# An inverse transform whose last stage contracts real and imaginary part at once, with channel-major rows

## The chip, the cores and the metric

The kernel runs on one core of one Trainium2 chip. The metric is the device time of one execution in microseconds; the median of several runs is given. The engines are named as in the profile: PE (matrix products; PEld is its weight loads), DVE (vector), ACT (scalar), POOL (GpSimd) and SP, which here only issues DMAs.

## The reference

Two layers on 2048 positions of 512 channels, each behind a layer norm and with a residual sum. The first is a long convolution whose kernel comes from 128 complex modes for each channel, done by Fourier transforms of length 4096; the second looks up one of 256 experts for each of 32 heads by the best of 16 keys in each of two halves.

```python
def _A_ref(u, log_A_real, A_imag, C_real, C_imag, log_dt, D_skip):
    L = u.shape[1]
    dt = jnp.exp(log_dt)
    A = -jnp.exp(log_A_real) + 1j * A_imag
    C = (C_real + 1j * C_imag) * dt[:, None]
    P = jnp.exp((A * dt[:, None])[:, :, None] * pos[None, None, :])
    K = 2.0 * jnp.einsum("dn,dnl->dl", C, P).real
    Kf, Uf = jnp.fft.rfft(K, 2 * L), jnp.fft.rfft(u_t, 2 * L)
    y = jnp.fft.irfft(Uf * Kf[None, :, :], 2 * L)[:, :, :L]
    ...
    return y + u * D_skip[None, None, :]

def _B_ref(x, w_q, k1, k2, u, v):
    q = jnp.einsum("nd,dhc->nhc", xf, w_q)
    s1, s2 = (jnp.einsum("nhd,ed->nhe", h, k) for h, k in ((q1, k1), (q2, k2)))
    ...                      # top 1 of 16 in each half, expert = 16 * i1 + i2
    act = _gelu(jnp.einsum("nd,nhkd->nhk", xf, ue))
    return jnp.einsum("nhk,nhk,nhkd->nd", g, act, ve)

h = x + _A_ref(_layernorm(x), ...)
h2 = h + _B_ref(_layernorm(h), ...)
```

## The kernel before

All work is added to a plan (`plan.add(engine, cost, function, ...)`): each step has an engine, an estimated cost, what it reads and writes, and the buffers it takes. `Plan.run` is a list scheduler on the host. It picks for each engine, in model time, the step of the highest rank among those that could start, and so writes the order of instructions on each engine; ranks are shifted by group through the weights in `BIAS`. On the chip each engine works off its own order and waits on semaphores. DMAs are issued by SP in such an order too.

**First half: the convolution.** The 512 channels are four quarters `c` of 128, in 32 groups `g` of four channels `d`. Transforms of 4096 are split in two stages over 32 by 64 frequencies. `factors` (POOL) and `tables` (ACT, DVE) make the modes' tables 16 channels at a time; `kgen` contracts them on PE into `kps` (L664), the convolution's kernel. `u_s1` and `k_s1` are the first stage for input and kernel (`stage1`, matmuls `s1u` and `s1k`, L448, evicted by ACT, L451), `u_s2` and `k_s2` the second (`stage2`, `s2yu` and `s2yk`, L465), whose moving operand is read out of a spectrum tile of 32 groups by 32 frequencies `k` by 4 channels. `k_s2` multiplies the spectra on DVE (`prod`, L701, L702, L704); in the last quarter ACT and POOL take a part (`part`, L708, and `rest`, L712). `k_ia` is the inverse's first stage (`ia`, L733), with 32 x 4 rows of frequency and channel; ACT evicts it into `T` (L738). For quarters 0 to 2 `T` is stored to DRAM as `t_d` (L744); the last quarter's stays in SBUF. As filler, `w_piece` folds keys into query weights (`wps`, `wpt`), stored as `w_d`.

**Handover.** The tables' buffers are closed (`turn_over`); the folded weights come back in four quarters `w_q` (L848), which ACT and DVE split into `w_hi` and `w_lo` (L851, L854).

**Second half: blocks of 256 positions, `b` = 0 to 7.** `prefetch` loads the block's part of `t_d` (`Tb`, L926), its constants (`cb`, two loads, L930) and the input (`xt`, L934), each into two buffers. `inverse` is the inverse's last stage (`ib`, L956): for each of 8 positions, two accumulating matmuls (real part, imaginary part) for each of four quarters, whose outputs lie in four column groups of the array. DVE adds the residual into `h` (L963). `center` and `variance` are the layer norm: `mean`, `hc` (L998), and its high and low part `hhi` (ACT, L1002) and `hlo` (DVE, L1006). `scores` multiplies by the weights (`sc`, L1062) and the experts' first vectors (`xu`, L1069), takes maxima (`mx`, `eq`, `kq`) and finds indices with POOL's help (`ks`, L1097, L1099; `ei`, `ef`, `ix`, L1104 to L1108). `select` counts experts by one-hot products (`oh`, `cnt`), weighs the second vectors (`o`, L1216), adds the residual (`ob`) and stores.

An FP32 matmul appears in the profile as two instructions.

Of the kernel before, what the change touches and what calls it, by code (L numbers as in the profile page):

```python
# [27 lines left out]
def view(t, off, dims):  # L28
# [5 lines left out]
BIAS = dict(cen0=483, cen1=-36, cen2=500, cen3=498, cen4=500, cen5=439, cen6=500, cen7=500, e1=216, ia0=470,  # L34
            ia1=333, ia2=6, ia3=40, inv0=452, inv1=500, inv2=309, inv3=479, inv4=407, inv5=104, inv6=64,
            inv7=500, k100=77, k101=254, k102=489, k103=419, k110=-5, k111=397, k112=327, k113=500, k120=481,
            k121=-358, k122=-122, k123=500, k130=500, k131=-78, k132=467, k133=497, k20=-230, k21=480, k22=500,
            k23=472, par=1000, par0=1000, par1=800, pre0=-182, pre1=7, pre2=-132, pre3=347, pre4=388, pre5=-110,
            pre6=273, pre7=456, sc0=363, sc1=495, sc2=488, sc3=434, sc4=110, sc5=462, sc6=277, sc7=500, sel0=14,
            sel1=454, sel2=487, sel3=209, sel4=478, sel5=497, sel6=497, sel7=-92, st=-12, tab0=286, tab1=-16,  # L40
            tab10=-139, tab11=364, tab12=484, tab13=146, tab14=476, tab15=431, tab16=99, tab17=456, tab18=500,
            tab19=227, tab2=273, tab20=435, tab21=459, tab22=-8, tab23=454, tab24=179, tab25=250, tab26=352,
            tab27=492, tab28=232, tab29=450, tab3=69, tab30=498, tab31=453, tab4=233, tab5=500, tab6=399,
            tab7=361, tab8=479, tab9=476, u100=77, u101=488, u102=303, u103=445, u110=500, u111=276, u112=-28,
            u113=492, u120=-167, u121=500, u122=443, u123=451, u130=491, u131=320, u132=-358, u133=491, u20=472,
            u21=207, u22=500, u23=497, var0=500, var1=431, var2=169, var3=336, var4=204, var5=442, var6=-355,
            var7=500, w0=281, w1=458, w2=-87, w3=367, w4=491, w5=362, w6=435, w7=202, wr=-122)
# [121 lines left out]
def kernel(ctx, tc, xa, xb, xt, lar, aim, cre, cim, ldt, dsk, wq, ka, kb, ue, ve,  # L169
# [14 lines left out]
    t_d = dram.tile([P, 8, 3, 2, 256], F32, name="t_d")  # L184
# [102 lines left out]
    def params():  # L287
# [128 lines left out]
        plan.add("SP", 0.1, lambda: nc.sync.dma_start(e_d, e1), r=["e1"], w=["e_d"], t=["e1"], lag=6.0)  # L416
# [23 lines left out]
    def stage1(dst, lhs8, kt, nm, r, tiles, key):  # L440
        for n in range(2):
            job = {}

            def mm(n=n, job=job):
                ps = bank(job, f"{nm}_{n}")
                for g in range(4):
                    for k in range(2):
                        T.matmul(ps[64 * k:64 * k + 64, g, :], lhs8(4 * n + g), c1_s[:, k], start=True, stop=True)  # L448

            def ev(n=n, job=job):  # L450
                A.copy(dst()[:, 8 * kt + 4 * n:8 * kt + 4 * n + 4].rearrange("p g k d -> p g (k d)"), job["ps"])  # L451

            k = plan.add("PE", 0.93, mm, r=r, t=tiles, take="psA", n_mm=16)
            plan.add("ACT", 0.48, ev, w=[key + (kt, n)], t=tiles, give="psA", after=[k])

    def stage2(c, nm, k4, deps, tiles):
# [3 lines left out]
        def mm():  # L460
            y = Q[c][nm]
            ps = bank(job, f"s2{nm}{c}_{k4}")
            for k in range(4):
                kk = 4 * k4 + k
                T.matmul(ps[:, k, :], c2_s[:, kk, :], y[:, :, kk, :], start=True, stop=True)  # L465
# [4 lines left out]
    def u_s1(c, kt):  # L470
# [16 lines left out]
        plan.add("SP", 0.1, load, w=[xs_k], t=[xs_k], lag=3.0)  # L487
# [85 lines left out]
    def factors(i, made):  # L573
# [17 lines left out]
        if i == 16:  # L591
            plan.add("SP", 0.1, e_load, r=["e_d"], w=["E1"], t=["E1"], lag=6.0)
# [97 lines left out]
    def k_s2(c):  # L690
# [3 lines left out]
        for k4 in range(8):  # L694
            job, k = stage2(c, "yk", k4, deps + [("U", c, k4)], tiles)

            def prod(job=job, k4=k4):
                yk, U = Q[c]["yk"], Q[c]["U"]
                pv = job["ps"].rearrange("p k (g d) -> p g k d", d=4)
                uv = U[:, :, 4 * k4:4 * k4 + 4]  # L700
                V.tensor_mul(yk[:, :, 4 * k4:4 * k4 + 4], pv, uv)  # L701
# [4 lines left out]
            def part(job=job, k4=k4):  # L706
                job["ki"] = wk.tile([P, 32, 4, 4], F32, tag="kt", name=f"ki{k4}", bufs=3)
                A.copy(job["ki"][0:64], job["ps"].rearrange("p k (g d) -> p g k d", d=4)[64:128])  # L708

            def rest(job=job, k4=k4):  # L710
                uv = Q[c]["U"][:, :, 4 * k4:4 * k4 + 4]
# [11 lines left out]
    def k_ia(c):  # L723
        plan.group = f"ia{c}"
        deps = [("P", c, k4) for k4 in range(8)]
        for n in range(8):
            job = {}

            def mm(n=n, job=job):
                ps = bank(job, f"ia{c}_{n}")  # L730
                for g in range(4):
                    for s, t in enumerate((Q[c]["yk"], Q[c]["U"])):
                        T.matmul(ps[:, g, :], t[:, 4 * n + g].rearrange("p k d -> p (k d)"), ca_s[:, s, :],  # L733
                                 start=(s == 0), stop=(s == 1))

            def ev(n=n, job=job):
                t_s = tile_of(Q[c], "T", lambda: con.tile([P, 128, 32], F32, tag="T", name=f"T{c}"))
                A.copy(t_s[:, :, 4 * n:4 * n + 4], job["ps"].rearrange("p g m -> p m g"))  # L738

            k = plan.add("PE", 1.80, mm, r=deps + ["ca"], t=[f"yk{c}", f"U{c}", f"T{c}"], take="psA", n_mm=16)  # L740
            plan.add("ACT", 0.55, ev, w=[("T", c, n)], t=[f"T{c}"], give="psA", after=[k])
        if c < 3:
            def store(r):
                nc.sync.dma_start(t_d[:, :, c, r],  # L744
                                  Q[c]["T"][:, 64 * r:64 * r + 64].rearrange("p (b m) g -> p b (m g)", b=8))

            for r in range(2):
                plan.add("SP", 0.1, lambda r=r: store(r), r=[("T", c, n) for n in range(8)], w=[("t_d", c, r)],
                         t=[f"T{c}"], lag=6.0)
# [3 lines left out]
    def w_piece(n):  # L753
# [32 lines left out]
        plan.add("SP", 0.1, load, w=[f"wq{n}"], t=[f"wq{n}"], lag=7.0)  # L786
# [4 lines left out]
        if q == 3:  # L791
            plan.add("SP", 0.1, store, r=[("wh", 4 * hg + j) for j in range(4)], w=[("w_d", hg)], t=[f"wh{hg}"],
# [48 lines left out]
    for q in range(4):  # L841

        if q:
            plan.ring(f"w_q{q}", f"w_q{q - 1}")

        def load(q=q):
            I["q"] = I["pre"].tile([P, 1024], F32, tag="wq", name=f"w_q{q}", bufs=1)
            nc.sync.dma_start(I["q"], w_d[:, q])  # L848

        def high(q=q):  # L850
            A.copy(I["hi"][:, q], I["q"])  # L851

        def low(q=q):
            V.tensor_sub(I["lo"][:, q], I["q"], I["hi"][:, q])  # L854

        plan.add("SP", 0.1, load, r=["pre"] + [("w_d", h) for h in range(8)], t=[f"w_q{q}"], w=[("w_q", q)], lag=6.0)
# [46 lines left out]
    plan.add("SP", 0.1, u_load, w=["u", "v"], lag=6.0)  # L903
# [16 lines left out]
    def prefetch(b):  # L920
# [3 lines left out]
        def load_t():  # L924
            t["T"] = I["pre"].tile([P, 3, 2, 8, 32], F32, tag="T", name=f"Tb{b}")
            nc.sync.dma_start(t["T"].rearrange("p c r m g -> p c r (m g)"), t_d[:, b])  # L926

        def load_c(a):
            t[f"cb{a}"] = I["pre"].tile([P, 4, 2, 128], F32, tag="cb", name=f"cb{b}_{a}")
            nc.sync.dma_start(t[f"cb{a}"], cb[:, 8 * b + 4 * a:8 * b + 4 * a + 4])  # L930
# [5 lines left out]
        for nm, n, fn, r in ((f"Tb", b, load_t, [("t_d", c, k) for c in range(3) for k in range(2)]),  # L936
                             ("cb", 2 * b, lambda: load_c(0), []), ("cb", 2 * b + 1, lambda: load_c(1), []),
                             ("xt", b, load_x, [])):
            k = key(nm, n)
            plan.add("SP", 0.1, fn, r=["pre"] + r, w=[k], t=[k], lag=6.0)  # L940

    def inverse(b):
# [3 lines left out]
        for a in range(2):  # L946
            job, kc = {}, f"cb{2 * b + a}"

            def mm(a=a, job=job):
# [386 lines left out]
```

## Time and profile before

| | us |
|---|---|
| median of 3 runs | 553.86 (552.82 to 553.98) |
| span of the profiled execution, first to last instruction | 549.5 |
| its own time beside the span | not shown on the page |
| PE busy | 471.7 (86%) |
| DVE busy | 418.6 (76%) |
| POOL busy | 325.5 (59%) |
| ACT busy | 296.4 (54%) |

The span is what the rows of the trace add up to; the device time holds what lies around it too. A busy PE in these rows is an engine with at least one product under way; as products overlap, the rate of starts within a group says more than the busy time. Groups of instructions are given as line, engine, operation, output from inputs, shapes and count, then busy us and mean ns of one, then the idle time before them and what ended it.

### The profile page before, as it was taken

To read this page: it belongs to the slowest core of one execution; us is meant where nothing else is said; L and a number is where in the kernel's file an instruction comes from. 1 tells how busy PE (TensorE), PEld (TensorE's weight loads), DVE (VectorE), ACT (ScalarE), POOL (GpSimd) and SP (SyncE) were. 2 spreads that over 40 slices of the span, in tenths; PEclk is the share of its full clock that TensorE was granted. 3 is DMA by queue.
4 is the path that set the end of the run, shared out by engine and by line. 5 is a ranking of instruction groups with operands and counts; after the bars stand their busy time and mean duration, and the time that the engine had idled before them with its cause. 6 is when DMAs were issued, how large, how long until landed. Compare 5 with 4: busy or idle time off the path is not lost.

```text
span 549.5 us, 16597 instructions
## 1 busy us (share of the span) xinstructions
PE 471.7 (86%) x7154; PEld 409.2 (74%) x7154; DVE 418.6 (76%) x698; ACT 296.4 (54%) x580; POOL 325.5 (59%) x339
## 2 busy tenths in 40 slices
PE   0023899989999999879987969999999999999996
PEld 0013788878999989869976968887888887877785
DVE  4999985899969987698537154788869595969975
ACT  5514998958898589829864334244043323323140
POOL 0758999999999999977607003470352515254500
PEclk9999999999999999989999999999999999999989
DMA  7962464672152031501067478300560503010002
GB/s 241 405 245 72 136 201 132 217 253 64 44 181 74 3 97 50 164 4 41 26 217 298 136 280 299 125 1 1 190 234 2 194 24 111 1 41 0 2 39 78
DMA packets 28481, 67.59 MB, mean 123 GB/s; under 512 B 2772, under 2 KB 14296, under 8 KB 28024
## 3 DMA queue, kind: packets, MB, share of 16 engines
q1 hardware_dynamic: 28256, 66.40, 34.8%
q8 instruction: 56, 0.92, 0.7%
q10 hardware_dynamic: 152, 0.13, 0.1%
q14 instruction: 17, 0.14, 0.1%
HBM read 52.50 MB, written 14.02 MB: 121 GB/s over the span
## 4 chain that ended last, share of the span: by engine, by line
PE 40%; DVE 9%; POOL 2%; issue 1%; DMA 1%; ACT 1%; DVEq 0%
PE sc L1062 13%; PE ia L733 6%; PE ib L956 5%; PE o L1216 5%; PE xu L1069 3%; PE cnt L1196 2%; PE s1k L448 1%; DVE eq L1086 1%; DVE mx L1082 1%; DVE oh L1186 1%; PE kps L664 1%; PE bc L1164 1%; DMA cb<-cb 1%; DVE yk L701 1%; POOL ks L1099 1%
## 5 line engine op out<-in xcount | busy, mean ns | idle before, releaser
L531 POOL TENSOR_TENSOR pg<-PS 128x1024 int32<-128x1024 int32 x32 | 68.8, 2152 | 3.6 <-ACT t L618 3.6
L560 POOL TENSOR_TENSOR mg<-TS 128x1024 f32<-128x1024 f32 x32 | 62.6, 1957 | 11.4 <-issue 4.3
L1186 DVE TENSOR_SCALAR oh<-idxb,ec_s 128x2048 bf16<-128x2048 bf16 (+1 forms) x72 | 49.9, 757 | 13.9 <-ACT idxb L1168 12.8
L1097 POOL TENSOR_TENSOR ks<-kq 128x512 f32<-128x512 bf16 x16 | 20.1, 1259 | 55.4 <-DVE kq L1091 54.8
L733 PE MATMUL ia<-ca_s,yk 128*128 128x128 f32 x256 | 51.5, 283 | 1.5 <-DVE yk L701 1.5
L733 PE MATMUL ia<-ca_s,U 128*128 128x128 f32 x256 | 50.6, 280 | 0.8 <-POOL U L712 0.8
L1062 PE MATMUL sc<-w_hi,hhi 128*128 128x512 f32 x128 | 43.7, 422 | 0.8 <-issue 0.5
L619 ACT ACTIVATE t<-t,halfpi 128x512 f32<-128x512 f32 x64 | 42.4, 662 | 2.1
L621 ACT ACTIVATE t<-pg 128x512 f32<-128x512 int32 x64 | 38.6, 610 | 7.8 <-POOL pg L531 6.3
L733 PEld LDWEIGHTS ia<-ca_s,yk 128*128 128x128 f32 x256 | 39.8, 196 | 2.8 <-DVE yk L701 1.7
L733 PEld LDWEIGHTS ia<-ca_s,U 128*128 128x128 f32 x256 | 39.8, 196 | 1.0 <-POOL U L712 1.0
L618 ACT ACTIVATE t<-pg 128x512 f32<-128x512 int32 x64 | 39.3, 614 | 2.4 <-DVE mg L638 1.6
L770 PE MATMUL wps<-wq,ka_s 128*32 128x128 f32 x256 | 15.0, 307 | 29.5 <-DMA wq<-wq 28.4
L1062 PE MATMUL sc<-w_lo,hhi 128*128 128x512 f32 x128 | 39.8, 392 | 0.0
L1062 PE MATMUL sc<-w_hi,hlo 128*128 128x512 f32 x128 | 39.6, 391 | 0.0
L465 PE MATMUL s2yk<-yk,c_s 128*128 128x128 f32 x256 | 33.8, 286 | 5.2 <-DVE U L704 4.2
L664 PE MATMUL kps<-mg 128*32 128x64 f32 x1024 | 34.1, 230 | 4.4 <-DVE mg L638 2.0
L563 POOL TENSOR_TENSOR mg<-TS 128x512 f32<-128x512 f32 x32 | 37.5, 1171 | 0.0
L465 PEld LDWEIGHTS s2yk<-yk,c_s 128*128 128x128 f32 x256 | 30.9, 197 | 7.7 <-PE s2yk L465 4.3
L465 PE MATMUL s2yu<-yu,c_s 128*128 128x128 f32 x256 | 33.0, 284 | 1.9 <-ACT yu L451 0.9
L956 PE MATMUL ib<-cb,Tb 128*32 128x128 f32 x768 | 31.4, 283 | 3.0 <-DMA cb<-cb 3.0
L465 PEld LDWEIGHTS s2yu<-yu,c_s 128*128 128x128 f32 x256 | 30.8, 196 | 4.0 <-ACT yu L451 1.2
(170 smaller groups left out, 1379.1 us busy)
## 6 DMA issues: line engine op xcount, KB each, us to landing
wq<-wq SPq DMA_DIRECT2D x32, 512.0 KB, 3.5
cb<-cb SPq DMA_DIRECT2D x16, 512.0 KB, 4.5
t_d<-T SPq DMA_DIRECT2D x6, 1024.0 KB, 8.9
Tb<-t_d SPq DMA_DIRECT2D x8, 768.0 KB, 6.5
x<-xa SPq DMA_DIRECT2D x8, 512.0 KB, 7.0
xs<-xb SPq DMA_DIRECT2D x16, 256.0 KB, 3.7
xt<-xt SPq DMA_DIRECT2D x8, 512.0 KB, 7.8
out<-ob SPq DMA_DIRECT2D x7, 512.0 KB, 2.7
```

The lines of the kernel that those rows point to most:

```text
L465: T.matmul(ps[:, k, :], c2_s[:, kk, :], y[:, :, kk, :], start=True, stop=True)
L531: G.tensor_tensor(view(pg, 0, [[32, 2 * NC], [8, 4], [1, 8]]), view(t["PS"], 1024 + off, [[1, 2 * NC], [128, 4], [0, 8]]), view(t["PS"], 8 ...
L560: G.tensor_tensor(view(mg, 0, [[96, NC], [8, 8], [1, 8]]), view(ts, 512 + 8 * o, [[8, NC], [1, 8], [0, 8]]), view(ts, 8 * o, [[8, NC], [0, ...
L563: G.tensor_tensor(view(mg, 64, [[96, NC], [8, 4], [1, 8]]), view(ts, 1536 + o, [[1, NC], [64, 4], [0, 8]]), view(ts, 1024 + 8 * o, [[8, NC ...
L618: A.activation(p, pg[:, :, k], AF.Abs)
L619: A.activation(p, p, AF.Sin, scale=-SINSCALE, bias=halfpi)
L621: A.activation(p, pg[:, :, k], AF.Sin, scale=SINSCALE)
L664: T.matmul(kps[32 * q:32 * q + 32, 2 * g + h, :], m[:, d, 64:96], m[:, d, 0:64], start=(e == 0), stop=(e == 1))
L733: T.matmul(ps[:, g, :], t[:, 4 * n + g].rearrange("p k d -> p (k d)"), ca_s[:, s, :], start=(s == 0), stop=(s == 1))
L956: T.matmul(ps[32 * c:32 * c + 32, j, :], t3[:, 64 * r + jj] if c == 3 else t_s[:, c, r, 4 * a + j], cbs[:, j, r, :], start=(r == 0), stop= ...
L1062: T.matmul(ps[:, 512 * h:512 * h + 512], t[x_][:, q, ts], I[w_][:, q, 512 * h:512 * h + 512], start=(q == 0 and x_ == w_), stop=(q == 3 an ...
L1186: V.tensor_scalar(oh[:, :, 0:ln], t["idxb"][:, :, sl], S["ec"][:, 4 * e + j:4 * e + j + 1], None, op0=ALU.is_equal)
```

## The change

The spectra are held as group, channel, frequency instead of group, frequency, channel; the constants `c1` and the views in `stage1`, `stage2`, `u_s2`, `prod`, `part`, `rest` and `k_ia` follow. The rows of `ia` are then channel-major, so that two channels of a group fill 64 rows. `T` is stored (four stores of 64 partitions for each quarter instead of two) so that 64 rows of real part and 64 of imaginary part of two channels lie under each other in the 128 partitions; in the last quarter the eviction does that turn itself, half on ACT, half on DVE, and the tile stays in SBUF. `ib` then contracts real and imaginary part in one matmul, two channels (`e`) at a time: as many matmuls, each with 64 moving columns instead of 128 and none accumulating. `cb` shrinks to a quarter, one load for each block. `inverse` is two steps of 32 instructions for each half block instead of one of 64. `w_q` has two buffers instead of one. The plan's cost of an SP step is 0.45 us instead of 0.1, and all weights in `BIAS` are new.

```diff
-            inv7=500, k100=77, k101=254, ... par=1000, par0=1000, par1=800, pre0=-182, ...
+            inv7=349, k100=-39, k101=41, ... par=1000, par0=147, par1=126, pre0=235, ...
...
-    t_d = dram.tile([P, 8, 3, 2, 256], F32, name="t_d")
+    t_d = dram.tile([P, 3, 2, 2048], F32, name="t_d")
...
-        return tile_of(Q[c], nm, lambda: wk.tile([P, 32, 32, 4], F32, tag=tag, name=f"{nm}{c}", bufs=2))
+        return tile_of(Q[c], nm, lambda: wk.tile([P, 32, 4, 32], F32, tag=tag, name=f"{nm}{c}", bufs=2))
...
-                T.matmul(ps[:, k, :], c2_s[:, kk, :], y[:, :, kk, :], start=True, stop=True)
+                T.matmul(ps[:, k, :], c2_s[:, kk, :], y[:, :, :, kk], start=True, stop=True)
...
-                A.copy(U[:, :, 4 * k4:4 * k4 + 4], job["ps"].rearrange("p k (g d) -> p g k d", d=4))
+                A.copy(U[:, :, :, 4 * k4:4 * k4 + 4].rearrange("p g d k -> p (g d) k"), job["ps"].rearrange("p k m -> p m k"))
...
-                pv = job["ps"].rearrange("p k (g d) -> p g k d", d=4)
-                uv = U[:, :, 4 * k4:4 * k4 + 4]
-                V.tensor_mul(yk[:, :, 4 * k4:4 * k4 + 4], pv, uv)
+                pv = job["ps"].rearrange("p k m -> p m k")
+                uv, kv = (t[:, :, :, 4 * k4:4 * k4 + 4].rearrange("p g d k -> p (g d) k") for t in (U, yk))
+                V.tensor_mul(kv, pv, uv)
...
+            def turn(copy, e, n=n, job=job):
+                pv = job["ps"].rearrange("p g (r m) -> p r m g", r=2)
+                for r in range(2):
+                    copy(tile_t()[64 * r:64 * r + 64, e, :, 4 * n:4 * n + 4], pv[64 * e:64 * e + 64, r])
...
-            plan.add("ACT", 0.55, ev, w=[("T", c, n)], t=[f"T{c}"], give="psA", after=[k])
+            if c < 3:
+                plan.add("ACT", 0.55, ev, w=[("T", c, n)], t=[f"T{c}"], give="psA", after=[k])
+            else:
+                a = plan.add("ACT", 0.70, lambda turn=turn: turn(A.copy, 0), w=[("T", c, n, 0)], t=[f"T{c}"], after=[k])
+                plan.add("DVE", 0.70, lambda turn=turn: turn(V.tensor_copy, 1), w=[("T", c, n, 1)], t=[f"T{c}"], give="psA",
+                         after=[k, a])
...
-            def store(r):
-                nc.sync.dma_start(t_d[:, :, c, r],
-                                  Q[c]["T"][:, 64 * r:64 * r + 64].rearrange("p (b m) g -> p b (m g)", b=8))
+        def store(r, e):
+            nc.sync.dma_start(t_d[64 * r:64 * r + 64, c, e],
+                              Q[c]["T"][64 * e:64 * e + 64, r].rearrange("p m g -> p (m g)"))
...
-            plan.ring(f"w_q{q}", f"w_q{q - 1}")
+            plan.ring(f"w_q{q}", f"w_q{q - 2}")
...
-            I["q"] = I["pre"].tile([P, 1024], F32, tag="wq", name=f"w_q{q}", bufs=1)
-            nc.sync.dma_start(I["q"], w_d[:, q])
+            I[f"q{q}"] = I["pre"].tile([P, 1024], F32, tag="wq", name=f"w_q{q}")
+            nc.sync.dma_start(I[f"q{q}"], w_d[:, q])
...
-        def load_c(a):
-            t[f"cb{a}"] = I["pre"].tile([P, 4, 2, 128], F32, tag="cb", name=f"cb{b}_{a}")
-            nc.sync.dma_start(t[f"cb{a}"], cb[:, 8 * b + 4 * a:8 * b + 4 * a + 4])
+        def load_c():
+            t["cb"] = I["pre"].tile([P, 8, 64], F32, tag="cb", name=f"cb{b}")
+            nc.sync.dma_start(t["cb"], cb[:, 8 * b:8 * b + 8])
...
-                for j in range(4):
-                    jj = 8 * b + 4 * a + j
-                    for r in range(2):
+                for j in js:
+                    m = 4 * a + j
+                    for e in range(2):
                         for c in range(4):
-                            T.matmul(ps[32 * c:32 * c + 32, j, :],
-                                     t3[:, 64 * r + jj] if c == 3 else t_s[:, c, r, 4 * a + j], cbs[:, j, r, :],
-                                     start=(r == 0), stop=(r == 1))
+                            T.matmul(job["ps"][32 * c:32 * c + 32, j, 64 * e:64 * e + 64],
+                                     t3[:, e, 8 * b + m] if c == 3 else t_s[:, c, e, 32 * m:32 * m + 32],
+                                     cbs[:, m], start=True, stop=True)
```

More of the change, by code (lines that the diff above doesn't have):

```diff
@@ L591, in factors @@
         if i == 16:
[L592 removed]
+            plan.add("SP", 0.45, e_load, r=["e_d"], w=["E1"], t=["E1"], lag=6.0)
         if i % 4 == 0 and i not in made:
@@ L791, in w_piece @@
         if q == 3:
-            plan.add("SP", 0.1, store, r=[("wh", 4 * hg + j) for j in range(4)], w=[("w_d", hg)], t=[f"wh{hg}"],
+            plan.add("SP", 0.45, store, r=[("wh", 4 * hg + j) for j in range(4)], w=[("w_d", hg)], t=[f"wh{hg}"],
                      lag=6.0)
@@ L965, in ev @@
                              t["xt"][:, :, sl].rearrange("p q (j l) -> p q j l", l=32))
-            k = plan.add("PE", 1.85, mm, r=["hp", kt_, kc] + [("T", 3, n) for n in range(8)] + [kx], t=[kt_, kc, kh, kx], take="psD", n_mm=64)
+            parts = [("T", 3, n, e) for n in range(8) for e in range(2)]
+            k = None
+            for js in ((0, 1), (2, 3)):
+                k = plan.add("PE", 0.58, lambda js=js, mm=mm: mm(js), r=["hp", kt_, kc, kx] + parts, t=[kt_, kc, kh, kx],
+                             take="psD" if k is None else None, after=[] if k is None else [k], n_mm=32)
             plan.add("DVE", 0.62, ev, r=[kx], w=[("h", b, a)], t=[kh, kx], give="psD", after=[k])
```

103 lines of the change are left out of this document (53 added, 50 removed).

## The prediction

> **What bounds the kernel now.** I read the page's totals first, then the busy time by stretch, then the chain of waits.
>
> ```profile
> span 549.5 us, 16597 instructions
> PE 471.7 (86%) x7154; PEld 409.2 (74%) x7154; DVE 418.6 (76%) x698; ACT 296.4 (54%) x580; POOL 325.5 (59%) x339
> ...
> 45.00:233.00 188.00, 174.83 (x3494) 158.12 (x3494) 157.90 (x275) 157.89 (x315) 180.58 (x166) 0.99 0.38 122
> 233.00:300.00 67.00, 58.18 (x994) 53.05 (x994) 49.30 (x79) 42.35 (x85) 41.36 (x32) 0.97 0.32 109
> 300.00:326.40 26.40, 21.99 (x262) 20.77 (x262) 7.70 (x12) 8.78 (x12) 0.28 (x1) 0.94 0.58 199
> 366.00:490.00 124.00, 123.67 (x1461) 100.96 (x1459) 97.42 (x135) 40.52 (x65) 49.21 (x67) 1.00 0.25 88
> 490.00:549.50 59.50, 51.46 (x503) 41.23 (x502) 44.34 (x70) 15.61 (x30) 15.69 (x20) 0.97 0.08 28
> ```
>
> In the rows by stretch the columns after the length are the busy times of PE, weight loads, DVE, ACT and POOL, then granted clock, DMA share and GB/s. Five limits follow one another. From 45 to 233 us POOL makes the tables (180.58 of 188 us) with PE close behind (174.83). To 300 us the last tables and the last quarter's spectrum drain. To 326 us PE works at a clock of 0.94 with 4.4 us of gaps: the handover to the second part. From 366 to 490 us PE is never out of work (123.67 of 124 us) and DVE has 79%. The end is a tail of waits. Work taken from PE counts fully in the fourth stretch, partly in the third, hardly in the tail.
>
> The chain of waits names the stage that the change touches (start, length, what):
>
> ```profile
> 271.90 1.03 PE kps L664 x64
> ...
> 316.34 0.59 ACT T L738
> 316.98 3.53 PE ib L956 x121
> 320.51 5.84 DMA cb<-cb
> 326.48 5.37 PE ib L956 x128
> ...
> 332.37 1.54 PE sc L1062 x6
> ...
> 337.53 3.63 PE ib L956 x128
> ...
> 388.98 3.63 PE ib L956 x128
> ...
> 400.39 3.63 PE ib L956 x128
> ...
> 430.10 3.63 PE ib L956 x128
> ...
> 483.57 3.63 PE ib L956 x128
> ```
>
> One block of 256 positions costs PE 3.63 us in 128 instructions (28.4 ns each). Seven of the eight blocks lie on the chain; the eighth lies beside a chain over DVE and POOL. The second block waits 5.84 us for its constants and then takes 5.37 us, because PE, having stood idle, is at reduced clock for a while.
>
> **Part one: half the columns.** The instruction count of `ib` stays (two contractions of 32 x 64 columns in place of two accumulating ones over real and imaginary part); each streams 64 columns instead of 128. The trace has that very form: `kps`, 128x32 weights, 64 columns, four column groups in turn.
>
> ```profile
> L664 PE MATMUL kps<-mg 128*32 128x64 f32 x1024 | 34.1, 230 | 4.4 <-DVE mg L638 2.0 <-issue 1.4 <-DVE gf L626 0.9
> ```
>
> On the chain 64 of these take 1.03 us, 16.1 ns each, weight loads included. So a block becomes 128 x 16.1 ns = 2.06 us, 1.57 us less. The five blocks on the chain from 337.53 on give 5 x 1.57 = 7.9 us. The block beside the chain is counted at nothing: what would hide it is the DVE and POOL work there, and if that cover goes it adds 1.57. Bounds: zero from below (a block is not dearer with fewer columns and the same loads), 6 x 1.57 = 9.4 from above.
>
> By the Trainium skill, "TensorE: Matmul & The Clock Gate", section "Wait — 56ns, not 53.3ns?", start-to-start never falls below about 25 ns however few the columns; that would make a block 128 x 25 = 3.2 us and five blocks worth only 2.1 us. The 16.1 ns of the `kps` row, in this form, is below that floor, so the row decides.
>
> **Part two: the handover.** Constants for a whole block now come in one transfer of 256 KB (64 columns for each of 8 positions) instead of two of 512 KB, two blocks ahead, so the second block's are there early; and the weights' quarters get two buffers.
>
> ```profile
> 307.16 6.96 SPq L848 DMA_DIRECT2D w_q<-w_d  x2
> ...
> 320.51 0.94 SPq L930 DMA_DIRECT2D cb<-cb  x2
> ...
> 322.55 0.38 SPq L848 DMA_DIRECT2D w_q<-w_d  x1
> ...
> 335.40 0.33 SPq L848 DMA_DIRECT2D w_q<-w_d  x1
> ```
> ```profile
> w_q<-w_d SPq DMA_DIRECT2D x4, 512.0 KB, 4.8
> ```
> ```profile
> 325.81 1.23 DVE L1006 TENSOR_TENSOR hlo<-hc,hhi 128x1024 fp32r<-128x1024 f32 x1
> ```
>
> Before, the second block's constants were issued at 320.51, only after the first block had freed the buffers, and SP stood 6.96 us over the first two weight quarters with everything else queued behind. After, the second block follows the first at once and runs in the time in which PE waited anyway. What is late next is the first block's own chain, whose last operand, `hlo`, ended at 327.04. It starts about 1.1 us earlier (1.57 from `ib`, less 0.4 for part three), but the third and fourth weight quarters now come through DVE just before it (one low part of about 1.2 us ahead of it). I take 327 for the first scores, against 332.37: 5.4 us. The quarters don't delay it further: the first two, issued at 307, land near 312, their parts are through and their buffers free near 315, and the last two, issued then, land 4.8 us later. The reduced clock then falls on the scores: the second block took 5.37 - 3.63 = 1.74 us more for it, so 1.7 is given back. Net 3.7 us; bounds 0 (the scores wait for something else as long) and 5.4.
>
> **Part three: the last quarter turned at eviction.** Eight evictions of 128x512 on ACT become two of 64x256 on ACT and two on DVE.
>
> ```profile
> L738 ACT COPY T<-ia 128x512 f32<-128x512 f32 x32 | 18.8, 588 | 18.5 <-PE ia L733 18.3
> L451 ACT COPY yu<-s1u 128x512 f32<-128x512 f32 x32 | 19.0, 597 | 4.2 <-PE s1u L448 4.1
> ...
> L1137 ACT COPY actT<-ta 128x256 f32<-128x256 f32 x16 | 5.5, 375 | 14.1 <-PE ta L1133 14.0
> ...
> L1204 DVE TENSOR_TENSOR wt<-cnt,actT 128x256 f32<-128x256 f32 x2 | 0.8, 420 | 0.4 <-PE cnt L1196 0.4
> ```
>
> Only the last one is on the path (the others fit under PE's next bank). ACT 2 x 375 = 750 ns and DVE 2 x 420 = 840 ns: 0.25 us later than 588 if they run side by side, 1.0 if one follows the other. 0.4 taken, within part two.
>
> **Part four: the channel-major layout.** It touches every first and second stage. The second stage's moving operand was runs of four neighbouring values (16 bytes); now each value is 128 bytes from the next.
>
> ```profile
> 291.14 3.84 PE L465 MATMUL s2yk<-yk,c_s 128*128 128x128 f32 x32
> ```
> ```profile
> L244 PE MATMUL mu<-st,eq 128*128 128x64 f32 x4 | 1.1, 423 | 9.4 <-DVE st L234 9.4
> L257 PE MATMUL va<-dv,eq 128*128 128x64 f32 x4 | 1.1, 428 | 0.3 <-ACT wh L781 0.3
> ```
> ```profile
> L1104 DVE TENSOR_SCALAR ei<-ks x16: 202/238/1165, 358.9 to 529.0; 128x64 int32<-128x64 int32 x16
> ```
> ```profile
> L314 DVE TENSOR_SCALAR RS<-pb 128x64 int32<-128x64 f32 x1 | 0.2, 198 | 0.0
> ```
>
> A stage-two instruction is 115 ns ((3.84 - 0.28)/31), 0.90 ns a column; there are 512. `mu` reads its moving values 24 bytes apart, `va` side by side: 423 and 428 ns, no dearer. But these eight ran at about half pace (423 ns against 230 for as many columns in `kps`), so they exclude only a pace slower than 1.8 ns a column. Bounds: 0 and 512 x 115 = 59 us. Nearer is DVE's read of values 32 bytes apart, 202 ns at its shortest against 198: no charge at about one value per ns. I take 0. The evictions of the second stage take the form that `T<-ia` has already (PSUM 512 bytes apart, runs of four out): 588 against 597 ns, nothing; the products on DVE read PSUM likewise, also taken at nothing.
>
> **Part five: stores and list.** The stores of `T` become four of 512 KB from 64 partitions each instead of two of 1 MB; SP issues six more, ahead of loads queued behind.
>
> ```profile
> 272.55 1.24 SPq L744 DMA_DIRECT2D t_d<-T  x2
> ...
> 291.81 0.33 SPq L926 DMA_DIRECT2D Tb<-t_d  x1
> ```
> ```profile
> t_d<-T SPq DMA_DIRECT2D x6, 1024.0 KB, 8.9
> ```
>
> They are issued 19 us before the first reload, land in 8.9, and so have 10 us of cover: 0. The new weights reorder everything. What they can find is seen in POOL's waits and at its start:
>
> ```profile
> 41.99 0.29 POOL L522 COPY PS<-A 128x128 int32<-128x128 int32 x1 [6.25 <-DVE A L334]
> ```
> ```profile
> POOL mg L560 <- PE kps L664: 4.0, 3, 3.5
> ```
>
> At best the 6.25 us in which POOL waited for the parameters, with PE's gaps; at worst as much or more. Zero taken, -8 to +12 kept for the range.
>
> **Sum.** 7.9 + 3.7 = 11.6 us off a span of 549.5: 537.9. The page gives no own time beyond the span; the runs' median of 553.86 is 4.4 above it, and I take that as what lies around it: 542.3, said as 542.
>
> **The rivals.** *Strided reads cost (slower).* Place: stage two, in the first half, where PE is the bound or just behind it. The price is 512 times the added ns; it decides from 11.6 us / 512 = 23 ns, that is 138 ns an instruction. At double, 59 us more: 601; a third of that, 562. For it: PE has 93% of its time taken from 45 to 233 us, so added time there finds little cover. Against it: the `mu` and DVE rows. By the Trainium skill, "SBUF — State Buffer", section "Door 1: The DMA port swizzle", lines are 16 bytes and every access to a new line pays a penalty; before, stage two read whole lines, after, one value of each. It names no price; the 202 ns of DVE's row disagree with it, and no row here shows PE at full pace.
>
> *The list makes the tables wait (slower).* POOL waits for a table buffer that PE frees in its own order: 3.5 us in the longest case. Four such waits more eat the gain; at six, 542 + 21 = 563. For it: POOL has 96% of its stretch, so there is more to lose than to win. Against it: PE has other work at hand there.
>
> *The list also wins the start.* The 6.25 us and a little of the gaps: 534.
>
> *The second half is not PE's alone.* With 8 us out of 124 DVE goes to about 84%, and waits for it take half of part one and part two: 548.
>
> **The chances.** Forecast 0.52; start won 0.10; half the gain 0.10; strided reads 0.13; tables waiting 0.12; all cancelling 0.03. No more than 0.2% (1.1 us) can be told from no change here. So faster 0.72, same 0.03, slower 0.25. The range, 532 to 562, leaves out most of the strided case and the tails of the others.
>
> **What would show it.** Right: `ib` of 64 columns at 2.0 to 2.2 us for 128 instructions; no wait for `cb`; first scores some 10 us after the last `T` eviction; stage two still near 115 ns; 366 to 490 still PE's, but shorter. Wrong: stage-two instructions starting more than 138 ns apart; POOL below 90% before 233; the last `ia` later than 316 by more than the gain; the second half's PE gaps growing by what `ib` saved.

## The result, and the profile after

The changed kernel takes 598.04 us (596.41 to 598.57, four runs) against 553.34 before: ratio 1.080 (1.076 to 1.084), slower by 44 us. I had forecast 542, with 532 to 562 as the range. The profiled execution took 596.41 us, 1.8 us more than its span. Ratios here and below leave out slowed executions; the profiled one of e10 was such, so its stages are not read.

The totals of the page after, and its busy time by stretch (columns as before: length, then PE, weight loads, DVE, ACT and POOL, granted clock, DMA share, GB/s):

```profile
span 594.6 us, 16632 instructions
PE 512.6 (86%) x7154; PEld 439.6 (74%) x7154; DVE 419.7 (71%) x714; ACT 299.0 (50%) x588; POOL 326.4 (55%) x339
...
45.00:233.00 188.00, 172.02 (x2821) 150.42 (x2822) 135.97 (x249) 121.52 (x248) 147.70 (x141) 0.98 0.37 113
233.00:300.00 67.00, 65.05 (x1001) 60.22 (x1000) 50.43 (x81) 46.44 (x86) 46.80 (x38) 1.00 0.15 37
...
366.00:490.00 124.00, 112.06 (x1408) 91.09 (x1409) 84.75 (x120) 41.77 (x62) 46.66 (x59) 0.94 0.32 106
```

PE has 41 us more to do (512.6 against 471.7) with the same 7154 instructions, though `ib` got cheaper. From 45 to 233 us POOL, which set the pace before with 180.58, is down to 147.70, and PE did 2821 instructions there instead of 3494 in about the same busy time: each is longer, and the tables wait for PE. The groups on PE say which are longer:

```profile
L465 PE MATMUL s2yu<-yu,c_s 128*128 128x128 f32 x256 | 59.4, 399 | 2.3 <-ACT yu L451 1.6 <-ACT U L501 0.7
L465 PE MATMUL s2yk<-yk,c_s 128*128 128x128 f32 x256 | 58.9, 399 | 0.4 <-ACT yk L451 0.4
L971 PE MATMUL ib<-cb,Tb 128*32 128x64 f32 x768 | 17.9, 232 | 5.9 <-DMA cb<-cb 5.9
L971 PE MATMUL ib<-cb,T 128*32 128x64 f32 x256 | 17.4, 232 | 1.8 <-DVE T L746 1.2 <-ACT T L746 0.6
```

The record of a stage-two instruction lasts 399 ns (284 to 286 before). How often one starts is read from an unbroken stretch of the timeline (start, length, what):

```profile
199.91 10.79 PE L465 MATMUL s2yk<-yk,c_s 128*128 128x128 f32 x48
```

(10.79 - 0.40)/47 = 221 ns each, against 115 before: nearly double. With 512 of them that is 54 us more on PE, 41 to 44 of which reach the end, as the runs below show. The rows that set where the two halves part are those of the last quarter's evictions, and of the handover's waits:

```profile
L746 ACT COPY T<-ia x16: 362/364/366, 351.5 to 364.7; 64x256 f32<-64x256 f32 x16
L746 DVE COPY T<-ia x16: 420/427/428, 352.3 to 366.2; 64x256 f32<-64x256 f32 x16
```
```profile
POOL mg L560 <- PE kps L664: 25.3, 10, 7.2
POOL pg L531 <- ACT t L618: 22.4, 5, 10.4
```
```profile
349.75 15.57 SPq L863 DMA_DIRECT2D w_q<-w_d  x4
...
372.39 0.58 SPq L945 DMA_DIRECT2D cb<-cb  x1
```
```profile
381.89 0.51 PE L971 MATMUL ib<-cb,Tb 128*32 128x64 f32 x4 [5.92 <-DMA cb<-cb]
...
385.65 0.73 PE L1081 MATMUL sc<-w_hi,hhi 128*128 128x512 f32 x1
```

Before, the last eviction of `T` ended at 316.9 us and 232.6 us followed; after, it ends at 366.6 (366.2 and one duration) and 228.0 follow. So the whole loss lies in the first half (+49.7), and the second half won only 4.6 of the 11.6 that I had given it. The first scores come 19.1 us after the last eviction (15.5 before): the new order puts `ib` of blocks 2 and 3 ahead of them, and PE stands 5.92 us in it for `cb`, which SP, held for 15.57 us by the four weight quarters, issued late. POOL's wait for PE's `kps` grew from 4.0 to 25.3 us.

### The profile page after: what moved, and what is told of

The parts are those of the page before. It is cut to its first block, busy times and chain, and to the rows that moved or that the text cites. A ratio compares the mean times of both kernels' runs of the same rounds, so it can differ in the third digit from the quotient of the medians.

```text
span 594.6 us, 16632 instructions
## 1 busy us (share of the span) xinstructions
PE 512.6 (86%) x7154; PEld 439.6 (74%) x7154; DVE 419.7 (71%) x714; ACT 299.0 (50%) x588; POOL 326.4 (55%) x339
## 5 line engine op out<-in xcount | busy, mean ns | idle before, releaser
L560 POOL TENSOR_TENSOR mg<-TS 128x1024 f32<-128x1024 f32 x32 | 62.7, 1960 | 33.5 <-PE kps L664 25.3
L465 PE MATMUL s2yu<-yu,c_s 128*128 128x128 f32 x256 | 59.4, 399 | 2.3 <-ACT yu L451 1.6
L465 PE MATMUL s2yk<-yk,c_s 128*128 128x128 f32 x256 | 58.9, 399 | 0.4 <-ACT yk L451 0.4
L465 PEld LDWEIGHTS s2yu<-yu,c_s 128*128 128x128 f32 x256 | 51.5, 211 | 7.1 <-ACT yu L451 2.3
L465 PEld LDWEIGHTS s2yk<-yk,c_s 128*128 128x128 f32 x256 | 51.4, 204 | 5.3 <-ACT yk L451 0.9
L1205 DVE TENSOR_SCALAR oh<-idxb,ec_s 128x2048 bf16<-128x2048 bf16 (+1 forms) x72 | 47.7, 733 | 5.2 <-ACT idxb L1187 5.2
L664 PE MATMUL kps<-mg 128*32 128x64 f32 x1024 | 32.7, 226 | 15.4 <-DVE mg L638 14.9
L1081 PE MATMUL sc<-w_hi,hhi 128*128 128x512 f32 x128 | 45.0, 431 | 0.5 <-issue 0.5
L625 DVE SCALAR_TENSOR_TENSOR gf<-mg,t 128x512 f32<-128x512 f32 x32 | 21.9, 684 | 27.7 <-ACT t L621 26.9
L664 PEld LDWEIGHTS kps<-mg 128*32 128x32 f32 x1024 | 24.0, 112 | 21.5 <-issue 17.6
```

Of the source, the lines that this page charges most:

```text
L465: T.matmul(ps[:, k, :], c2_s[:, kk, :], y[:, :, :, kk], start=True, stop=True)
L560: G.tensor_tensor(view(mg, 0, [[96, NC], [8, 8], [1, 8]]), view(ts, 512 + 8 * o, [[8, NC], [1, 8], [0, 8]]), view(ts, 8 * o, [[8, NC], [0, ...
L625: V.scalar_tensor_tensor(gf[:, :, up], mg[:, :, up], -1.0, p, op0=ALU.mult, op1=ALU.mult)
L664: T.matmul(kps[32 * q:32 * q + 32, 2 * g + h, :], m[:, d, 64:96], m[:, d, 0:64], start=(e == 0), stop=(e == 1))
L1081: T.matmul(ps[:, 512 * h:512 * h + 512], t[x_][:, q, ts], I[w_][:, q, 512 * h:512 * h + 512], start=(q == 0 and x_ == w_), stop=(q == 3 an ...
L1205: V.tensor_scalar(oh[:, :, 0:ln], t["idxb"][:, :, sl], S["ec"][:, 4 * e + j:4 * e + j + 1], None, op0=ALU.is_equal)
```

## The experiments

Theory A: the strided moving operand of stage two is the loss; runs of two values, 8 bytes, would end it. Rivals: the new list is the loss; the evictions and products are. Two questions came later: where the forecast's gain is once the stride is gone, and what part one is worth.

Each run with its ratio to the kernel before, the end of the last eviction of `T` (last start and one duration) and the rest of the span:

| run | us | ratio (95%) | `T` ends | after that |
|---|---|---|---|---|
| before | 553.3 to 555.5 | 1 | 316.9 | 232.6 |
| after | 598.04 | 1.080 (1.076 to 1.084) | 366.6 | 228.0 |
| e2 pairs | 553.61 | 1.000 (0.997 to 1.003) | 322.6 | 228.6 |
| e3 layout only | 594.70 | 1.076 (1.069 to 1.083) | 356.4 | 235.4 |
| e5 old weights | 590.84 | 1.067 (1.064 to 1.070) | 342.6 | 245.1 |
| e6 scores first | 558.04 | 1.007 (1.004 to 1.010) | 320.5 | 230.8 |
| e7 four `cb` | 552.43 | 0.997 (0.994 to 1.000) | 321.5 | 226.4 |
| e8 old weights, four `cb` | 593.77 | 1.072 (1.069 to 1.075) | 343.0 | 247.7 |
| e9 first half as before | 557.18 | 1.006 (1.003 to 1.009) | 316.2 | 239.2 |
| e10 new weights alone | 593.84 | 1.070 (1.066 to 1.075) | | |
| e11 two lists | 545.97 | 0.984 (0.980 to 0.988) | 315.2 | 228.3 |
| e12 `ib` twice | 567.95 | 1.023 (1.019 to 1.027) | 315.7 | 252.4 |
| e13 `ib` wide | 550.92 | 0.994 (0.992 to 0.996) | 314.4 | 234.1 |

### Paces of a strided operand (e1)

Groups of 48 products (96 FP32 instructions, 48 of bf16), 128 columns, 128x128 weights, on an otherwise idle core; what changes is where the moving values lie, or the weights:

```python
run("side", wc, lambda i: x[:, 128 * (i % 32):128 * (i % 32) + 128])
run("four", wc, lambda i: x4[:, :, i % 32, :])      # runs of 4
run("pair", wc, lambda i: x2[:, :, i % 32, :])      # runs of 2
run("lone", wc, lambda i: x1[:, :, i % 32])         # one value, 128 bytes apart
run("gap2", wc, lambda i: every(x, 2))              # every 2nd value; 3, 4, 6 alike
...
run("wgtl", lambda i: w1[:, :, i % 32], lambda i: x[:, 0:128])
run("hgap2", whc, lambda i: every(xh, 2))           # bf16; 4, 8 alike
```

> This kernel leaves out the whole computation: it only times 48 FP32 products (96 instructions) of 128 columns for each of 16 forms of operand. Theory A, one 16-byte line of the moving operand per step, two values of a line needed for full pace: side (neighbouring values), four (runs of four) and pair (runs of two) and gap2 (8 bytes apart) start every 110 to 120 ns; gap4, gap6 and lone (16, 24 and 128 bytes apart) every 220 to 230 ns; gap3 (12 bytes apart) between. Rival B, every read that is not a whole line costs: pair and gap2 are at 220 to 230 ns too, or at least over 150. Rival C, the stride is not the cause in the changed kernel: all of them at 110 to 120 ns. For weights 16 and 128 bytes apart (wgt4, wgtl) A expects either no change, if weight loads stay hidden behind products, or up to 230 ns.

The timeline of ACT: each eviction starts when the last product of its group is done, so the difference from one start to the next is the time of a group. The four of `gap` are 2, 3, 4 and 6, the three of `hgap` 2, 4 and 8, and `wgt` reads every fourth weight:

```profile
25.52 0.59 ACT L46 COPY o<-warm 128x512 f32<-128x512 f32 x1 [14.76 <-PE warm L45]
...
36.24 0.59 ACT L46 COPY o<-side 128x512 f32<-128x512 f32 x1 [10.13 <-PE side L45]
...
46.96 0.59 ACT L46 COPY o<-four 128x512 f32<-128x512 f32 x1 [10.13 <-PE four L45]
...
57.69 0.59 ACT L46 COPY o<-pair 128x512 f32<-128x512 f32 x1 [10.14 <-PE pair L45]
...
78.80 0.59 ACT L46 COPY o<-lone 128x512 f32<-128x512 f32 x1 [20.52 <-PE lone L45]
89.68 0.59 ACT L46 COPY o<-gap 128x512 f32<-128x512 f32 x1 [10.30 <-PE gap L45]
106.32 0.59 ACT L46 COPY o<-gap 128x512 f32<-128x512 f32 x1 [16.05 <-PE gap L45]
128.08 0.59 ACT L46 COPY o<-gap 128x512 f32<-128x512 f32 x1 [21.17 <-PE gap L45]
...
149.84 0.59 ACT L46 COPY o<-gap 128x512 f32<-128x512 f32 x1 [21.18 <-PE gap L45]
...
170.83 0.59 ACT L46 COPY o<-wgtl 128x512 f32<-128x512 f32 x1 [20.40 <-PE wgtl L45]
...
193.23 0.59 ACT L46 COPY o<-wgt 128x512 f32<-128x512 f32 x1 [21.82 <-PE wgt L45]
...
195.91 0.59 ACT L46 COPY o<-hside 128x512 f32<-128x512 f32 x1 [2.09 <-PE hside L45]
198.68 0.59 ACT L46 COPY o<-hgap 128x512 f32<-128x512 f32 x1 [2.19 <-PE hgap L45]
204.25 0.59 ACT L46 COPY o<-hgap 128x512 f32<-128x512 f32 x1 [4.98 <-PE hgap L45]
...
215.13 0.59 ACT L46 COPY o<-hgap 128x512 f32<-128x512 f32 x1 [10.30 <-PE hgap L45]
```

| group | ns an instruction | 16-byte lines touched |
|---|---|---|
| side, four, pair | 112 | 32, 32, 64 |
| gap 2 | 113 | 64 |
| gap 3 | 173 | 96 |
| gap 4, gap 6, lone | 227, 227, 220 | 128 |
| weights one value a line (`wgtl`, `wgt`) | 219, 233 | moving 32 |
| bf16 side, gap 2 | 56, 58 | 16, 32 |
| bf16 gap 4 | 116 | 64 |
| bf16 gap 8 | 227 | 128 |

Divide by the lines: wherever the stride of the moving values costs anything, it comes to 1.72 to 1.81 ns for each line of 16 bytes touched (220/128, 227/128, 173/96, 116/64). An FP32 column alone takes 0.88 ns, so two in a line hide it; a bf16 column takes 0.44, so two in a line (116 ns) don't hide it and four (58) do. Distance shows no part in it: every fourth value costs what every sixth does, and values 128 bytes apart no more. So theory A holds, and rivals B and C of this run fall. The Trainium skill, "Advanced Engine Details and Errata", section "Memory Cachelines", asks for at least two hits on a 16-byte line and says that the tolerance depends on the data type. The trace agrees for FP32; for bf16 it finds two hits too few and four enough.

Nor does the price of a line follow the clock. The granted clock fell in the course of the last bf16 group (`hgap` 8) and came back in the group behind it, FP32 side by side. The first two rows are of `hgap` 8, the last two of the group behind it (after the length, busy time and instructions of PE, weight loads, DVE, ACT and POOL, then the granted clock):

```profile
205.00:207.00 2.00, 2.00 (x11) 1.00 (x10) 0.00 (x0) 0.00 (x0) 0.00 (x0) 1.00 0.00 0
211.00:213.00 2.00, 2.00 (x11) 1.10 (x9) 0.00 (x0) 0.00 (x0) 0.00 (x0) 0.50 0.00 0
215.10:217.10 2.00, 2.00 (x11) 2.00 (x11) 0.00 (x0) 0.59 (x1) 0.00 (x0) 0.50 0.00 0
221.00:223.00 2.00, 2.00 (x21) 2.00 (x20) 0.00 (x0) 0.00 (x0) 0.00 (x0) 1.00 0.00 0
```

At one value in a line, as many instructions pass in 2 us at half the clock as at the full one; side by side it is 11 against 21. At half the clock the stride can hardly be seen.

### The layout alone, and pairs (e3, e2)

e3 is the kernel before with channel-major spectra and nothing else; its `cb` rows are reordered to fit.

```diff
-        return tile_of(Q[c], nm, lambda: wk.tile([P, 32, 32, 4], F32, tag=tag, name=f"{nm}{c}", bufs=2))
+        return tile_of(Q[c], nm, lambda: wk.tile([P, 32, 4, 32], F32, tag=tag, name=f"{nm}{c}", bufs=2))
...
-                T.matmul(ps[:, k, :], c2_s[:, kk, :], y[:, :, kk, :], start=True, stop=True)
+                T.matmul(ps[:, k, :], c2_s[:, kk, :], y[:, :, :, kk], start=True, stop=True)
```

> The kernel before with its own order, and of the change the channel-major spectra alone (last stage as before). Theory A: stage two at 225 ns, up to 57 us more: 595 to 611 us, little hidden because PE has few gaps in the first half. Rival C (order): under the old order at most half of it shows, under 580 us. No effect of the stride: 553.

e2 is the changed kernel with two channels side by side: group, channel pair, frequency, channel of the pair. Rows stay such that two channels fill 64 of them, and all other parts of the change stay.

```diff
-        return tile_of(Q[c], nm, lambda: wk.tile([P, 32, 4, 32], F32, tag=tag, name=f"{nm}{c}", bufs=2))
+        return tile_of(Q[c], nm, lambda: wk.tile([P, 64, 32, 2], F32, tag=tag, name=f"{nm}{c}", bufs=2))
...
-                T.matmul(ps[:, k, :], c2_s[:, kk, :], y[:, :, :, kk], start=True, stop=True)
+                T.matmul(ps[:, k, :], c2_s[:, kk, :], y[:, :, kk, :], start=True, stop=True)
```

> The changed kernel with the same order of instructions, its spectra held as group, channel pair, frequency, channel of the pair: 64 rows still hold two channels, and the second stage's moving operand comes in runs of two values. Theory A (one line per step, two values suffice): stage two back at 113 to 117 ns an instruction, 512 x 111 = 57 us less PE work, of which the first half showed 48: 545 to 552 us. Rival B (only whole lines are at full pace): stage two stays over 150 ns, 565 to 598 us. Rival C (the new order of instructions delays the tables, stage two only fills the gaps): pace restored but the time stays over 580 us.

Stage two on the timeline of e3, and then of e2:

```profile
199.55 10.79 PE L465 MATMUL s2yu<-yu,c_s 128*128 128x128 f32 x48
```
```profile
182.78 5.91 PE L465 MATMUL s2yk<-yk,c_s 128*128 128x128 f32 x48
```

221 ns each in e3, (5.91 - 0.28)/47 = 120 in e2. The layout alone costs 41 us on the old list and without any other part (ratio 1.076); taking the stride away gives 44 us back on the new one. That settles the loss. e3's evictions and products cost what they did (`U<-s2yu` 586 ns against 592, `yk<-s2yk` 689 against 689), so this rival falls. The two times lie just beside theory A's ranges (594.70 against 595 to 611, 553.61 against 545 to 552), the paces in them. Between e2 and after, `T` ends 44.0 us apart and the second halves are 0.6 apart: the stride's price lies in the first half. But e2 stands where the kernel before stands: the 11.6 us are not there. Its first half is 5.7 us longer than before, its second half 4.0 us shorter. A run with the spectra as before and strided weights of `ia` (e4) gave no result, so strided weights are measured in e1 alone.

### Old weights, the order, four buffers (e5 to e8)

e5 puts the old numbers into `BIAS` of e2. e6 gives the first `ib` step of block 2 `after=[...]` the last score step of block 0. e7 changes buffers only:

```diff
-                 actT=2, ixT=2, idxb=2, wt2=2, ob=1, Tb=2, cb=2, xt=2)
+                 actT=2, ixT=2, idxb=2, wt2=2, ob=1, Tb=2, cb=4, xt=2)
...
-            I[f"q{q}"] = I["pre"].tile([P, 1024], F32, tag="wq", name=f"w_q{q}")
+            I[f"q{q}"] = I["pre"].tile([P, 1024], F32, tag="wq", name=f"w_q{q}", bufs=1)
```

> The kernel of the run before (spectra with pairs of channels side by side, 553.6 us, ratio 1.000), with the weights of the list as they were before the change. Everything else of the change stays: 64 columns in ib, the turn at eviction, one load of cb for a block, two buffers for w_q. Theory (the new list gives back what parts one and two win): with the pairs, the last eviction of T ended at 322.6 us against 316.9 before and the scores began some 20 us after it against 15.5; with the old weights both come back, and the time is 542 (538 to 546). Rival (the parts are worth less than their sum, whatever the list, because DVE and the transfers take PE's place): 549 to 554. Second rival (the old weights suit only the old kernel): above 556.

> The same kernel with pairs and the new weights; the only edit is that the ib of block 2 is put behind the scores of block 0 in the plan. In the run with pairs PE stood 8.2 us in ib for cb of block 2, with the scores of block 0 behind it in its order. Theory (that order costs the handover its gain): no wait for cb of more than 1 us before the first score, the first score 5 to 7 us earlier against the last eviction of T, and the time 546 to 549. Rival (hlo or the u loads hold the scores just as long): first score no more than 2 us earlier, 552 to 554. Second rival (ib of blocks 2 and 3 later leaves PE without work in the middle): the first score earlier, the time unchanged.

> The same kernel with pairs and the new weights; cb has four buffers in place of two and w_q one in place of two (the memory is that of before). The loads of cb for blocks 2 and 3 need then wait for no buffer. Theory (the wait for cb is one of buffers): the 8.2 us wait goes, ib of blocks 2 and 3 fills PE's time before the first score, 546 to 550. Rival (the wait is one of transfers: Tb of block 2, in two buffers and behind the u loads in SP's order, comes as late): the wait is named Tb instead and the time is 552 to 555.

> Both edits: pairs, the weights of the list as before, four buffers for cb and one for w_q. If the list is what costs, this is within 2 us of the run with the old weights alone; if the wait for cb is what costs, it is 4 to 8 us below it. With neither, 549 to 554.

e5: 590.84, its second rival. The old weights do not bring the old order back, since costs and buffers in the plan changed with the list; `T` ends 20 us later than in e2 and the second half is 16.5 longer. e8 is the same with e7's buffers, and no better (2.9 us above e5, outside each of its cases).

e6: its theory fails. The wait for `cb` is gone and the first scores start at 332.0, 11.5 us after the last eviction instead of 20.0 in e2, yet the time is 4 us longer, not shorter (the profiled execution, 551.3 us of span, was the fastest of ten). Nearest is its second rival: from 366 to 490 us PE is at work for 119.71 us, against 121.19 in e2.

e7: the wait for `cb` goes, and another takes its place, as its rival had it; from the waits of PE:

```profile
PE ib L971 <- DMA Tb<-t_d: 6.5, 1, 6.5
```

It is 0.3% below e2, which can't be told from none: each of the two ratios is known to 0.3%.

### The list taken apart (e9, e10, e11)

e9 has pairs, the old weights, and the plan's old costs and buffers (SP steps 0.1, the four stores 0.05 each, one `w_q`). e10 is the kernel before with the new weights. e11 ranks the steps up to the handover by the old weights and costs and those behind it by the new ones, with e7's buffers:

```diff
+        rank, first = ranks(self.bias, 9.0)
+        first[:self.half] = ranks(BIAS0, 0.1)[1][:self.half]
```

> Spectra with pairs of channels side by side; weights of the list and costs of SP steps as before, one buffer for w_q as before. In this form the order of PE's instructions up to the last ia is that of the kernel before, group for group; behind it stand 64 columns in ib, one cb for a block, the turn at eviction. In the run with the old weights alone (590.8 us) costs and buffers were those of the change, and the list came out otherwise: the last eviction of T ended at 342.6 us. Theory (a set of weights is only as good as the plan that it was drawn for; the parts themselves win): the last eviction of T at 317 to 318 us, as before, the second half 226 to 229 us instead of 232.6, the time 545 to 549, below before by 5 to 9 us. My first sum, 542, asks for a second half of 221. Rival (the order behind the handover goes wrong too without new weights): the second half 235 or more, the time 552 or more.

> The kernel before with nothing but the new weights. If the new weights are a worse list in themselves, this is 555 to 565 us, the first half some 5 us longer as in the run with pairs. If weights fit only their own plan, as the 590.8 us of the old weights on the new plan suggest, this is 570 to 600. If they are a better list in themselves: 548 or less.

> Pairs; steps up to the handover ranked by the weights before (SP's costs as before), steps behind it by the new weights (SP's costs as changed); four buffers for cb, one for w_q. PE's order is then that of the kernel before up to the last ia, and behind it that of the run with four buffers for cb. If the two halves add: last eviction of T at 315.8 us (as measured with the first half as before), second half 226.8 (as measured with four buffers for cb), span 542.6, time 546 to 548, ratio 0.986 to 0.990. If the second half loses again what it starts earlier (its transfers then begin earlier too, among the stores of T and of the folded weights): 551 or more.

e9: the first half is back (`T` ends at 316.2), but the second takes 239.2: its rival. The third weight quarter comes late, and the scores, begun early, stop for it; from the chain of waits of e9:

```profile
325.95 9.40 DMA w_q<-w_d
...
394.40 1.92 PE ib L971 x128
```

e10: 593.84, 7% slower. So each set of weights costs 37 to 40 us on the other's plan: by these two runs neither is a better or worse list in itself, each fits one plan.

e11: 545.97 us, ratio 0.984 (0.980 to 0.988), faster than both kernels: by 8.8 us against before (1.6% of 554), by 52 against after. The two halves add up as expected: 315.2 and 228.3.

### What part one is worth (e12, e13)

Both stand beside e11. e12 issues every `ib` matmul twice; e13 keeps their number and order, and seven of eight stream their columns twice:

```diff
-                                     cbs[:, m], start=True, stop=True)
+                                     cbs[:, m].unsqueeze(1).to_broadcast([P, n, 64]), start=True, stop=True)
```

> The run beside it with every matmul of ib issued twice (the second writes the same values over the first; the order of all other work unchanged), some 1.9 us of PE more for each of 8 blocks, 15.4 us in all: about what the change took away from ib's 3.63 us a block. Theory of the prediction (five of eight blocks lie on the path, PE's time counts in full there): 9 to 11 us longer than the run beside it. Rival (the second half isn't PE's alone; half or less of the saving arrives): 4 to 7 us longer. Second rival (none on the path): under 2 us.

> The kernel of the two lists (ratio 0.984) with as many instructions in ib and the same order, but seven of eight of them stream their 64 columns twice, into 128 columns; what is written too much is written over by the next one, the last of each bank stays at 64. So ib alone goes back towards its 128 columns, about 1.5 us of PE for each of eight blocks, 12 us in all. (In the run with every matmul issued twice PE stood 16.9 us in ib with no cause shown, so that its 22 us can't be put down to columns.) Theory of the prediction (five or six of eight blocks on the path): 7 to 9 us more than 546, so 553 to 555, ratio 0.996 to 1.001. Rival (the second half isn't PE's alone): 549 to 551, ratio 0.988 to 0.993. Second rival (part one is worth nothing here, the gain came from the handover): 545 to 547.

e12 took 22 us more, above every case, and is no measure of columns: from the waits of PE, in e12,

```profile
PE ib L991 <- issue: 16.9, 8, 5.0
```

that is, eight stops of up to 5.0 us in `ib` for which the profile shows nothing that PE waited for; e11 has one such stop of 2.8 us. What they are stays open.

e13: `ib` in 380 to 390 us of e11, and in 380 to 392 of e13 (busy time of these instructions alone):

```profile
380.00:390.00 10.00, 1.99 (x128) 1.83 (x128) 1.28 (x2) 1.00 0.37 125
```
```profile
380.00:392.00 12.00, 3.49 (x128) 3.33 (x128) 1.38 (x2) 1.00 0.45 154
```

1.50 us more a block, 12.0 in all. The ratio goes from 0.984 to 0.994, about 5.4 us (3.0 to 7.8), 45% of what PE got. That is nearest the rival (0.988 to 0.993; the theory asked for 0.996 or more), but the interval's upper end touches the theory's 7 to 9. Of the eight blocks three lie in the handover, where the first scores start at 335.0 against 334.6; and from 366 to 490 us PE is at work for 123.11 us in e13 and 121.66 in e11, so part of what it saves becomes waiting.

## Why the prediction was wrong

**The step that failed** is part four: "I take 0", between ends of 0 and 59 us. The other end was nearly right, 54 us of PE time, of which 41 to 44 reached the end; the rival "Strided reads cost (slower)", priced at 601 for double, is what happened (598.04), and I gave it 0.13. That 601 came so near is partly luck: it took off a gain of 11.6 us that was not there (e2: ratio 1.000) and put on 59 us where 41 to 44 arrived. Both rows that argued it away could not speak. `mu` ran at half pace, so a column took as long as a line does, 1.8 ns, and nothing could show, as in the half-clock rows of e1. I said as much, and then let DVE's row decide as the "nearer" one: another engine, and no price for PE's. The sentence on 16-byte lines from the Trainium skill, "SBUF — State Buffer", section "Door 1: The DMA port swizzle", which I let these rows outweigh, was right: two hits a line asked for, one given, and 221 ns instead of 115.

**Part one** was right in its price and perhaps too high in its worth. A block takes 1.92 us (2.06 forecast), 15.0 ns an instruction: below the 25 ns floor that I quoted from the Trainium skill, "TensorE: Matmul & The Clock Gate", section "Wait — 56ns, not 53.3ns?", so there the row was rightly preferred. Worth: 5.4 us for 7/8 of it, 6.2 for the whole by that share (3.4 to 8.9), against 7.9; the noise leaves room for both.

**Part two** failed in what is late next. I had the scores 10 us after the last `T`; with the new order they come 19 to 20 us after it in after, e2 and e11, more than the 15.5 before. When they did come early (e6, e9), nothing was gained: `hlo` was there, but the next weight quarter (e9) or, as far as PE's busy time tells, work for the middle (e6) was not. The granted clock was the other term set too small. In the 40 us behind the last `T`, in the kernel before and in e2 (columns as before):

```profile
316.90:356.90 40.00, 35.57 (x497) 31.36 (x498) 23.67 (x26) 13.05 (x15) 10.32 (x11) 0.96 0.64 233
```
```profile
322.60:362.60 40.00, 31.06 (x485) 27.08 (x486) 20.20 (x26) 11.66 (x14) 9.06 (x10) 0.83 0.50 164
```

PE stands 4.5 us more there, and its clock gives some 5 us less ((0.96 - 0.83) x 40, an estimate), where I had given 1.7 back. No run takes the clock apart from the waits, so its share of the missing gain stays open.

**Part three**: 1.6 us a bank (two ACT copies of 364 ns, then two DVE copies of 427) instead of 0.59. The halves follow one another, as the `after=[k, a]` of the change orders them, the case that I had put at 1.0; I took 0.4.

**Part five**: 0, "-8 to +12". In e2 the new list lets `T` end 5.7 us later, and a set of weights on a plan that isn't its own costs 37 to 40. The range was too narrow for a step that reorders everything. The rival on tables that wait had the right place: POOL waits 12.9 us for `kps` in e2, 4.0 before.

**The base** was off as well: I took 4.4 us around the span, but e2, e11 and after all show 1.8. By that the profiled execution of before was some 2.6 us faster than the median.

Without the stride and with each half on its own list (e11), the rest of the change gains 8.8 us (6.8 to 10.9), where I forecast 11.6. The size is near, the make-up is not the one forecast: e11 has four buffers for `cb` and one for `w_q`, its first scores come late and PE waits 6.1 us for `Tb`. Of the 8.8 us e13 gives some 5.4 to the columns of `ib`; what the rest is made of no run shows.

## What to carry to other kernels

When a layout turns a matmul's moving operand (or its weights) from runs into single values, count the 16-byte lines that it touches and take 1.8 ns each where that is more than the columns cost (0.88 ns each in FP32, 0.44 in bf16), or keep runs of two FP32 or four bf16 values. A row that bounds a cost must have run at the pace and on the engine in question. Tuned weights of a list scheduler belong to one plan: after any edit of costs or buffers, compare the order before the times.

## What was not expected of the hardware

- A strided read by PE is paid by the line, 1.72 to 1.81 ns, alike for FP32 and bf16 and alike at a granted clock of 1.00 and 0.50 (bf16, every 8th value); the distance between values plays no part (every 4th and every 6th: 227 ns).
- Weights with one value in a line slow a 128-column FP32 product as much as moving values do: 219 to 233 ns against 112.
- ACT and DVE read PSUM with values 512 bytes apart at no charge over runs of four (586 against 592 ns, 689 against 689).
- With 256 instead of 128 `ib` instructions in a row (e12), PE stood eight times, 16.9 us in all, without a releaser in the profile; the cause stays open.
